# Half-height turns in large groups, inverse rows in another PSUM pool, and one forward transform with four residues

## Chip, core and metric

The kernel runs on one core of a Trainium2 chip. The metric is the device time of one execution in microseconds (us); of several runs the median counts. The engines are TensorE (PE in the profile, with PEld for its weight loads), VectorE (DVE), ScalarE (ACT), GpSimd (POOL) and SyncE (SP, which here issues DMAs only). PSUM, in which TensorE writes and from which ScalarE and VectorE read, has eight banks.

## What is computed

The reference is the forward pass of a gated block and the gradients of a loss with respect to nine of its inputs. With S = 2048 rows, D = 1024 channels and F = 3584:

```
xn = layernorm(q)                                  # 2048 x 1024
kv = shift_conv(k, shift_k) * v                    # 4 taps along the rows
y  = irfft(rfft(kv, 4096) * rfft(ssm_k, 4096))[:2048] + kv * ssm_D
g  = silu(((xn @ w_gate) * (xn @ w_up)) @ w_down)
out = q + (xn * y) * g
```

and then the gradients of q, k, v, shift_k, ssm_k, ssm_D, w_gate, w_up and w_down for a given gradient of out. All tensors are bf16.

## The kernel before

All work is on one core, in one program. TensorE does the large matrix products one after the other; the long convolution runs beside them, as pieces of work that are put between the matmuls.

**Forward stage (to about 513 us of the span).** The rows of q come in chunks, are normalised on VectorE, and are turned (transposed) on TensorE so that the channels lie on the partitions (`layer_norm`, L564 to L612; the last two chunks of four row blocks in `turn_late`, L614 to L619). `gu_unit` (L640 to L694) then does one unit: a slab of 256 columns of w_gate and w_up against four row blocks (two, or one, at the start). Each row block is eight matmuls of 512 columns into a PSUM tile `psg` (L656), which ScalarE copies to `gut` (L658). After a unit, VectorE multiplies the two halves into `hN` (in `multiply`), GpSimd stores hN, and `turn` (L684 to L694), deferred by five row blocks, turns the eight 128x128 blocks of hN with eight transposes on TensorE (L689) into one bank of `ps_tr`, ScalarE copies them to `hT` (L691), and SyncE stores 256 KB of hT to `HTd`. There are 14 slabs of four units.

A transpose here is a matmul: the block is loaded as weights, and the identity, 128 columns, streams through.

**Convolution (between the units).** `conv_forward` (L701 to L883) is a generator that is advanced by `tick` after every row block; the planner `make_pump` spreads its steps evenly by prices written beside each `yield`, which are DVE times less 0.95 of the TensorE time that the step adds (`pe_us`, `net`). Eight channel slices of 128 go through it. Per slice: two forward transforms, that of the filter h (with the D row added to it) and that of kv; a product in frequency; an inverse transform. A forward transform is done in two halves. A half is matmuls of 256 columns against a table into PSUM tiles `psF` (two buffers of two banks, pool `ps_cv`, L235), ScalarE copies of 1024 elements to `SP`, and sums and differences on VectorE. It exists in two forms: with four residues (`fwd4_half`, 16 matmuls a half; eight VectorE instructions of 1024 elements in all) and with eight (`fwd8_half` and `fwd8`, 8 matmuls a half; more VectorE instructions). `EIGHT` lists which (slice, kind) use the second; kind 0 is kv, kind 1 is h. The inverse ends in rows (`tail`): `inv8_rows` (L446) or `inv_rows` (L457) multiply two residues at a time into the single-bank tile `psY` (pool `ps_y`), ScalarE copies 512 elements to `yf` (L773), four times a slice. Before its transform, h of the next slice is turned by `h_rows` (L743 to L759): sixteen 128x128 blocks in two calls of eight (L752 and L754), each into the single buffer of `ps_tr`, each with a ScalarE copy (L755). The source of these blocks has a step of eight elements between columns. `turn_tables` (L186 to L195) turns the tables for the inverse, once.

**PSUM in this stage:** ps_y one bank, ps_tr one, psg two, and four for `ps_st` in the layer norm, which later become the two buffers of ps_cv.

**After it (513 us on).** The product with w_down (`bm_mm`, L994), the gates, and the last rows of the inverse of slice 7, whose four steps are put behind late matmuls 52, 55, 58 and 61 (`at`); then the whole backward pass, up to 1916 us. The order of instructions on each engine follows the program's order as a scheduler places it; instructions of the convolution on VectorE keep theirs.

Of the kernel before, what the change touches and what calls it, by code (L numbers as in the profile page):

```python
# [19 lines left out]
def build_kernel(  # L20
# [12 lines left out]
    P = 128  # L33
# [152 lines left out]
    def turn_tables(psp):  # L186

        for j in range(2):
            for rq in range(2):
                ps = psp.tile([P, 4, 2, P], BF16, name="psY")  # L190
                for i in range(4):
                    for k in range(2):
                        nc.tensor.transpose(ps[:, i, k, :], T4[j][:, 4 * rq + i, k, :], ident[:])
                nc.scalar.copy(out=TI[:, j, 4 * rq:4 * rq + 4], in_=ps[:])
                yield  # L195
# [253 lines left out]
    def inv_rows(G, psp, rp):  # L449

        ps = psp.tile([P, 2, 256], F32, name="psY")
        for i in range(2):
            r = 2 * rp + i
            n = 0
            for j in range(2):
                for k in range(2):
                    nc.tensor.matmul(ps[:, i, :], TI[:, j, r, k, :], gseg(G, r, j, k),  # L457
                                     start=(n == 0), stop=(n == 3))
                    n += 1
        return ps  # L460
# [67 lines left out]
    busy = ps_st.tile([P, 4, P], F32, name="tr")  # L528
# [35 lines left out]

    def layer_norm(b0, n, x4):
# [22 lines left out]
        for i in range(n):  # L588
            b = b0 + i
            q, qi = divmod(b, 4)  # L590
            last = V.tensor_scalar(x4[:, i, :], x4[:, i, :], mv[:, i, 0:1], RSTD[:, b:b + 1], op0=SUB, op1=MUL)
            if b < 2:
                for hh in range(2):
                    ps = ps_st.tile([P, 4, P], BF16, name="tr")
# [3 lines left out]
                    act_copy[0] = nc.scalar.copy(out=XNT[0][:, 4 * hh:4 * hh + 4, b * P:b * P + P], in_=ps[:])  # L598
# [10 lines left out]
            act_copy[0] = nc.scalar.copy(out=XNT[q][:, :, qi * P:(qi + 1) * P], in_=ps[:])  # L609
# [3 lines left out]
    def turn_late():  # L613
        for i, (x, q, qi) in enumerate(turn_rows):  # L614
            ps = ps_st.tile([P, DC, P], BF16, name="tr")
            for dc in range(DC):
                tr_ln[0] = nc.tensor.transpose(ps[:, dc, :], x[:, dc * P:(dc + 1) * P], ident[:])
            act_copy[0] = nc.scalar.copy(out=XNT[q][:, :, qi * P:(qi + 1) * P], in_=ps[:])
        turn_rows.clear()  # L619
# [4 lines left out]
    gu_mm = [None]  # L624

# [12 lines left out]
    chunk = [0]  # L638

    def gu_unit(sl, b0, n, w, tick):  # L640
# [26 lines left out]
        def multiply():  # L667
            with tc.issue_after(last.ins) if b0 + n <= 4 and chunk[0] <= 2 else nullcontext():
                by_half = lambda t: t.rearrange("p i (a f) -> p a i f", a=2)
                tt(hN[:, :, 0:n], by_half(gut[:, 0, 0:n]), by_half(gut[:, 1, 0:n]), MUL)  # L670
            st(Hd[sl][:, :, b0:b0 + n, :], hN[:, :, 0:n])
            defer(turn)
        hn[0] = multiply

        def store(hT):
# [3 lines left out]
            if n == 4:  # L679
                ht_st[0] = ld(to[q0:q0 + 2].rearrange("q f a s -> f q (a s)"), hT[:].rearrange("f q a i s -> f q (a i s)"))  # L680
            else:
                ht_st[0] = ld(to[q0, :, :, i0 * P:(i0 + n) * P], hT[:, 0, :, 0:n].rearrange("f a i s -> f a (i s)"))

        def turn():  # L684
            hT = fg.tile([P, 2, 2, 2, P], BF16, name="hT") if chunk[0] > 5 else lnp.tile([P, 2, 2, 2, P], BF16, name="hT_s", bufs=5)
            ps = ps_tr.tile([P, 2, 2, 2, P], BF16, name="tr")
# [3 lines left out]
            if n == 4:  # L690
                nc.scalar.copy(out=hT[:], in_=ps[:])  # L691
# [4 lines left out]
    h_out = []  # L696
    ht_st = [None]
    EIGHT = ((0, 0), (0, 1), (5, 0), (6, 0), (7, 0), (7, 1))
# [7 lines left out]
    def conv_forward():  # L706
# [36 lines left out]
        def h_rows(ds, c):  # L743
# [3 lines left out]
            if c == 0:  # L747
                S_["hx"] = cf.tile([P, NB, P], BF16, name="hx")
            pe_us[0] += 0.47
            ps = ps_tr.tile([P, 8, P], BF16, name="tr")  # L750
            with tc.issue_after(tr_ln[0].ins):
                nc.tensor.transpose(ps[:, 0, :], hrow[:, c, :, 0], ident[:])  # L752
            for r in range(1, 8):
                nc.tensor.transpose(ps[:, r, :], hrow[:, c, :, r], ident[:])  # L754
            nc.scalar.activation(S_["hx"][:, 8 * c:8 * c + 8, :], ps[:], ACT.Copy, scale=WSC)  # L755
            if c == 1:
                h_out.append(ds)
                if ds + 1 < 8:
                    load_h(ds + 1)  # L759
# [4 lines left out]
        def tail(ds):  # L764
# [5 lines left out]
            for rp in range(4):  # L770
                ps = (inv8_rows if ds in INV8 else inv_rows)(G, ps_y, rp)
                pe_us[0] += 0.45 if ds in INV8 else 0.9
                nc.scalar.copy(out=by_res(yf, rp), in_=rowps(ps))  # L773
                if ds == 7 and rp < 2:
                    nc.scalar.copy(out=y_first[0][:, 2 * rp:2 * rp + 2, 7 * P:8 * P], in_=yf[:, 2 * rp:2 * rp + 2])
                if rp == 3:
# [50 lines left out]
        h_rows(0, 0)  # L827
        h_rows(0, 1)
        yield 0.1
        tl = turn_tables(ps_y)  # L830
        sp = [half(0, S_["hx"], i, Dz[:, 0:P]) for i in range(2)]
        for ds in range(8):
# [16 lines left out]
            next(tl, None)  # L849
            room = cf.tile([P, 4, 256], F32, name="room", tag="hx")[:] if eight else None  # L850
            yield from transform(ds, int(ds > 0), sph, HX if ds else KX, room, nop1 if eight else lambda c: h_rows(ds + 1, c),
                                 lambda: next(tl, None))
            if ds == 0:
                S_["kst"] = st(KFd[0], KX[:])
            if eight:
                h_rows(ds + 1, 0)
            turned(HX, 1, 0, 1)
            yield 1.3
            if eight:
                h_rows(ds + 1, 1)  # L860
# [24 lines left out]
    F_TOTAL = 4 * SHIFT_W + 3.0 + 8 * (0.5 + FWD4_W + 1.3 + PROD_W + INV_W) + 10.0 - 0.95 * 8 * (4 * 1.75 + 0.95 + 4 * 0.9)  # L885
# [121 lines left out]
    ps_cv.release()  # L1007
    ps_bm = pool("ps_bm", 2, side="right", space=PSUM)
# [246 lines left out]
    def gate(b, ps, parts=None):  # L1255
# [23 lines left out]
        def turn():  # L1279
            ps = ps_tr.tile([P, DC, P], BF16, name=tr_name[0])  # L1280
            for dc in range(DC):
                nc.tensor.transpose(ps[:, dc, :], dbm[:, dc * P:(dc + 1) * P], ident[:])
            nc.scalar.copy(out=DBMT[b // 4][:, :, (b % 4) * P:(b % 4 + 1) * P], in_=ps[:])
# [53 lines left out]
    at = (52, 55, 58, 61)  # L1337
    for n in range(at[3] + 1):
# [27 lines left out]
    done = at[3] + 1  # L1366
# [35 lines left out]
    for p_ in (ps_bx, ps_tr, ps_y, ps_bm, mi, mo, mt, mh[1], mh[0]):  # L1402
# [364 lines left out]
```

## Time and profile before

| what | value |
|---|---|
| median of 3 runs | 1919.29 us (1917.67 to 1920.26) |
| profiled execution, span from first to last instruction | 1916.6 us |
| granted TensorE clock, mean | 1.000 |
| PE busy | 1905.7 us (99%), 10915 matmuls |
| DVE busy | 1557.1 us (81%) |
| ACT busy | 640.0 us (33%) |
| POOL busy | 334.5 us (17%) |

The span is 2.7 us shorter than the median of the runs. A row of a timeline gives the start of a group in us, its length, engine, line, operation, the tile written and read, the shapes and how many instructions were merged; a bracket at the end gives the engine's idle time before it and what ended that. Neighbouring matmuls overlap at their ends, so what one costs is the distance between the starts of two groups over the count of the first, not its length. In a row of stretches, each engine's busy time is followed by its number of instructions.

### The profile page before, as it was taken

To read this page: it belongs to the slowest core of one execution; us is meant where nothing else is said; L and a number is where in the kernel's file an instruction comes from. 1 tells how busy PE (TensorE), PEld (TensorE's weight loads), DVE (VectorE), ACT (ScalarE), POOL (GpSimd) and SP (SyncE) were. 2 spreads that over 40 slices of the span, in tenths; PEclk is the share of its full clock that TensorE was granted. 3 is DMA by queue.
4 is the path that set the end of the run, shared out by engine and by line. 5 is a ranking of instruction groups with operands and counts; after the bars stand their busy time and mean duration, and the time that the engine had idled before them with its cause. 6 is when DMAs were issued, how large, how long until landed. Compare 5 with 4: busy or idle time off the path is not lost. (4 is left out here: it accounts for less than half of the span.)

```text
span 1916.6 us, 27330 instructions
## 1 busy us (share of the span) xinstructions
PE 1905.7 (99%) x10915; PEld 1024.9 (53%) x10915; DVE 1557.1 (81%) x1723; ACT 640.0 (33%) x946; POOL 334.5 (17%) x465
## 2 busy tenths in 40 slices
PE   8999999999999999999999999999999999999999
PEld 5555555545544456666666665664444444444444
DVE  8999999999997556887999999999995205788862
ACT  5864555646433233432222222222222102011121
POOL 5121212111113220001031221111212101111120
PEclk9999999999999999999999999999999999999999
DMA  8776867668679997677887698585787999999962
GB/s 293 271 261 216 265 209 234 211 234 299 237 246 287 316 287 250 205 240 236 269 271 261 220 263 270 180 286 177 217 255 173 206 205 191 184 184 195 193 180 97
DMA packets 425487, 444.28 MB, mean 232 GB/s; under 512 B 268784, under 2 KB 343180, under 8 KB 410896
## 3 DMA queue, kind: packets, MB, share of 16 engines
q1 hardware_dynamic: 367888, 239.03, 46.9%
q0 software_dynamic: 41152, 174.15, 29.1%
q10 hardware_dynamic: 16320, 29.36, 4.1%
q8 instruction: 85, 1.39, 0.3%
q14 instruction: 42, 0.34, 0.1%
HBM read 193.87 MB, written 189.84 MB: 200 GB/s over the span
## 5 line engine op out<-in xcount | busy, mean ns | idle before, releaser
L656 PE MATMUL psg<-wslab,U 128*128 128x512 bf16 x1792 | 407.3, 379 | 3.0 <-DMA wslab<-in_B_w_gate_dram 2.0
L1458 PE MATMUL psb<-U,U 128*128 128x512 bf16 x1792 | 397.1, 379 | 0.0
L1603 PE MATMUL psx<-U,dgut 128*128 128x512 bf16 x1536 | 333.0, 379 | 0.5 <-DVE dxn L213 0.5
L1603 PEld LDWEIGHTS <-dgut 128*128 128x128 bf16 x1792 | 175.3, 98 | 212.1 <-issue 0.8
L1458 PEld LDWEIGHTS <-U 128*128 128x128 bf16 x1792 | 175.2, 98 | 198.0
L656 PEld LDWEIGHTS <-U 128*128 128x128 bf16 x1792 | 172.2, 98 | 187.4 <-issue 2.5
L1441 PE MATMUL psb<-wdt,U 128*128 128x256 bf16 x1792 | 205.6, 273 | 0.0
L213 DVE TENSOR_TENSOR W<-W 128x1024 f32<-128x1024 f32 (+1 forms) x192 | 189.1, 1001 | 4.2
L1441 PEld LDWEIGHTS <-U 128*128 128x128 bf16 x1792 | 175.3, 98 | 29.2
L1541 PE MATMUL psb<-U,U 128*128 128x512 bf16 x816 | 177.3, 379 | 0.0
L1463 ACT CAST wb<-psb 128x512 bf16<-128x512 f32 x112 | 65.6, 586 | 315.4 <-PE psb L1458 310.5
L1208 DVE SCALAR_TENSOR_TENSOR dkp<-dkT,kT 128x1024 bf16<-128x1024 bf16 (+2 forms) x64 | 78.3, 1224 | 104.0 <-DMA dkT<-DKSHd 102.2
L994 PE MATMUL psbm<-U,ht 128*128 128x512 bf16 x672 | 146.0, 379 | 0.0
L1541 PEld LDWEIGHTS <-U 128*128 128x128 bf16 x896 | 87.4, 98 | 104.3
L658 ACT CAST gut<-psg 128x512 bf16<-128x512 f32 x156 | 91.3, 588 | 120.0 <-PE psg L656 119.1
L1635 ACT ACTIVATE dx_t<-dxn 128x1024 bf16<-128x1024 f32 x15 | 15.9, 1057 | 324.2 <-DVE dxn L213 320.3
L994 PEld LDWEIGHTS <-ht 128*128 128x128 bf16 x672 | 65.6, 98 | 78.0
L213 DVE TENSOR_TENSOR U<-U,dht 128x2048 bf16<-128x2048 bf16 x56 | 68.3, 1221 | 46.4 <-ACT dht L1443 46.4
L1443 ACT CAST dht<-psb 128x512 bf16<-128x512 f32 x112 | 65.6, 587 | 116.3 <-PE psb L1441 116.3
L66 POOL DMA_DIRECT2D Hd<-hN x54 | 37.1, 686 | 292.3 <-DVE hN L213 289.4
L1582 ACT CAST wbs<-psb 128x512 bf16<-128x512 f32 x51 | 29.9, 586 | 145.4 <-PE psb L1541 137.3
L213 DVE TENSOR_TENSOR W<-SP 128x1024 f32<-128x1024 f32 x64 | 74.5, 1219 | 2.5 <-ACT SP L296 1.7
(261 smaller groups left out, 2386.3 us busy)
## 6 DMA issues: line engine op xcount, KB each, us to landing
U<-GUd SPq DMA_DIRECT2D x28, 1024.0 KB, 8.7
DGd<-U SPq DMA_DIRECT2D x28, 1024.0 KB, 6.5
GUd<-gut ACTq DMA_DIRECT2D x39, 512.0 KB, 5.5
out_dram<-wb SPq DMA_DIRECT2D x112, 128.0 KB, 4.8
U<-Hd SPq DMA_DIRECT2D x14, 1024.0 KB, 5.9
Hd<-hN POOLq DMA_DIRECT2D x54, 256.0 KB, 4.2
HTd<-hT SPq DMA_DIRECT2D x52, 256.0 KB, 3.9
ht<-HTd SPq DMA_DIRECT2D x18, 512.0 KB, 7.7
```

What stands on the lines that cost most here:

```text
L66: ins = nc.gpsimd.dma_start(out=out, in_=in_)
L213: pinned(V.tensor_tensor(o, a, b, op))
L656: gu_mm[0] = nc.tensor.matmul(ps[:], XNT[q][:, dc, qi * P:(qi + 1) * P], w[:, dc].rearrange("p a f -> p (a f)"), start=(dc == 0), stop=(dc ...
L658: nc.scalar.copy(out=gut[:, :, i], in_=ps[:].rearrange("p (a f) -> p a f", a=2))
L994: mm = nc.tensor.matmul(ps[:, dh * 512:(dh + 1) * 512], ht(fc)[:, i * P:(i + 1) * P], WD[fc // 4][:, fc % 4, dh * 512:(dh + 1) * 512], sta ...
L1208: ins = V.scalar_tensor_tensor(prod[:].rearrange("p r d -> p (r d)")[:, lo:H], dkT[:, 0, lo:H], 1.0, kT[:, 0, 13 + m + lo:13 + m + H], op0 ...
L1441: nc.tensor.matmul(ps[:, x * SLW:(x + 1) * SLW], DBMT[2 * hf + g][:, dc, (b % 4) * P:(b % 4 + 1) * P], wdt[:, dc, :], start=(dc == 0), sto ...
L1443: nc.scalar.copy(out=dht[:, 2 * e:2 * e + 2].rearrange("p b f -> p (b f)"), in_=ps[:])
L1458: nc.tensor.matmul(ps[:], XN[b // 4][:, b % 4, dc * P:(dc + 1) * P], dgus[b // 8][:, :, b % 8], start=(b == 0), stop=(b == NB - 1))
L1463: nc.scalar.copy(out=wb[:, dc % 2].rearrange("p a f -> p (a f)"), in_=ps[:])
L1541: nc.tensor.matmul(ps, h[:, f, b, :], DBM[b // 4][:, b % 4, dh * 512:(dh + 1) * 512], start=(b == 0), stop=(b == NB - 1))
L1603: nc.tensor.matmul(ps[:, dh * 512:(dh + 1) * 512], t[n][:, f, i * P:(i + 1) * P], WGU[n][:, f, dh * 512:(dh + 1) * 512], start=(n == 0 and ...
```

## The change

1. **Turns by halves of the rows.** A transpose of a 128x128 block becomes two of 64x128: partitions 0 to 63 and 64 to 127 are turned by two matmuls on separate halves of the array's rows, each with a 64x64 identity, so 64 columns stream through; the two results go to different banks. This is done where many turns stand together: hN of slabs 2 to 13, where the two units of a half of the rows are now kept (`mate`) and turned together as 16 blocks (`turn_pair`); all sixteen blocks of h in one call; and the 32 blocks of each late chunk (`turn_late`). `ps_tr` becomes two banks, still one buffer; hT becomes one buffer of double size, stored with one DMA of 512 KB.
2. **Inverse rows.** The pool ps_y goes. `inv_quad` does four residues at a time into a buffer of psF (after the end of ps_cv: into ps_tr), with ScalarE copies of 1024 elements, twice a slice. The tables are turned there too, in two groups of 16.
3. **kv of slice 5** leaves EIGHT and is transformed with four residues.
4. The last rows of slice 7, now two steps, stand behind late matmuls 62 and 69. The planner's price for TensorE of turning h goes from twice 0.47 to 0.67.

In number of instructions: 576 transposes of 128 columns become 1152 of 64, with as many weight loads; 16 matmuls of 256 columns are added; VectorE loses 10 tensor_tensor and 4 scalar_tensor_tensor of 512 elements and gains 2 tensor_tensor of 1024; 48 stores of hT become 24; 32 copies of inverse rows become 16.

```diff
     def turn_tables(psp):
...
-            for rq in range(2):
-                ps = psp.tile([P, 4, 2, P], BF16, name="psY")
...
+            ps = psp.tile([P, 8, 2, P], BF16, name="psT", tag="psF")
...
-    def inv_rows(G, psp, rp):
...
+    def inv_quad(G, ps, rq, eight):
+
+        for i in range(4):
+            r = 4 * rq + i
             n = 0
-            for j in range(2):
+            for j in range(1 if eight else 2):
                 for k in range(2):
...
-    ps_y = pool("ps_y", 1, space=PSUM)
...
-    ps_st = pool("ps_st", 4, space=PSUM)
...
+    ps_st = pool("ps_st", 1, space=PSUM)
+    turns = ps_st.tile([P, 4, 2, 4, P], BF16, name="tr")
...
+    def turn_halves(ps, src):
+
+        for hh in range(2):
+            rows = slice(64 * hh, 64 * hh + 64)
+            ins = nc.tensor.transpose(ps(hh), src[rows], ident[rows, rows])
+        return ins
...
     def turn_late():
+        ps = turns[:].rearrange("p (h j) i b x -> p h j i (b x)", h=2).rearrange("p h j i (a u) -> p h (j i) a u", u=64)
         for i, (x, q, qi) in enumerate(turn_rows):
-            ps = ps_st.tile([P, DC, P], BF16, name="tr")
             for dc in range(DC):
-                tr_ln[0] = nc.tensor.transpose(ps[:, dc, :], x[:, dc * P:(dc + 1) * P], ident[:])
...
+                tr_ln[0] = turn_halves(lambda hh: ps[:, hh, i, dc], x[:, dc * P:(dc + 1) * P])
...
+    def tr_tile():
+        return ps_tr.tile([P, 2, 8, P], BF16, name="tr")
...
-            defer(turn)
+            if sl < 2:
+                defer(turn)
+            else:
+                mate.append(hN)
+                if b0 % 8 == 4:
+                    defer(turn_pair)
...
+        def turn_pair():
+            hT = fg.tile([P, 4, 2, 2, P], BF16, name="hT", bufs=1)
+            two_, mate[:] = mate[0:2], mate[2:]
+            ps = tr_tile()[:].rearrange("p h b x -> p h (b x)").rearrange("p h (b u) -> p h b u", u=64)
+            for qq in range(4):
+                for a in range(2):
+                    for i in range(2):
+                        turn_halves(lambda hh: ps[:, hh, 4 * qq + 2 * a + i], two_[qq // 2][:, a, qq % 2 * 2 + i, :])
+            to = HTd[b0 // 8][sl // 4][:, :, 2 * (sl % 4):2 * (sl % 4) + 2, :]
+            for g in range(2):
+                nc.scalar.copy(out=halves(hT[:, 2 * g:2 * g + 2].rearrange("p q a i s -> p (q a i) s")), in_=ps[:, :, 8 * g:8 * g + 8])
+            ht_st[0] = ld(to.rearrange("q f a s -> f q (a s)"), hT[:].rearrange("f q a i s -> f q (a i s)"))
...
-    EIGHT = ((0, 0), (0, 1), (5, 0), (6, 0), (7, 0), (7, 1))
+    EIGHT = ((0, 0), (0, 1), (6, 0), (7, 0), (7, 1))
...
-        def h_rows(ds, c):
+        def h_rows(ds):
...
-            pe_us[0] += 0.47
-            ps = ps_tr.tile([P, 8, P], BF16, name="tr")
+            pe_us[0] += 0.67
+            ps = tr_tile()[:].rearrange("p h b x -> p h (b x)").rearrange("p h (b u) -> p h b u", u=64)
             with tc.issue_after(tr_ln[0].ins):
-                nc.tensor.transpose(ps[:, 0, :], hrow[:, c, :, 0], ident[:])
-            for r in range(1, 8):
-                nc.tensor.transpose(ps[:, r, :], hrow[:, c, :, r], ident[:])
-            nc.scalar.activation(S_["hx"][:, 8 * c:8 * c + 8, :], ps[:], ACT.Copy, scale=WSC)
...
+                turn_halves(lambda hh: ps[:, hh, 0], hrow[:, 0, :, 0])
+            for b in range(1, 16):
+                turn_halves(lambda hh: ps[:, hh, b], hrow[:, b // 8, :, b % 8])
+            for c in range(2):
+                nc.scalar.activation(halves(hx[:, 8 * c:8 * c + 8, :]), ps[:, :, 8 * c:8 * c + 8], ACT.Copy, scale=WSC)
...
-            for rp in range(4):
-                ps = (inv8_rows if ds in INV8 else inv_rows)(G, ps_y, rp)
...
+            for rq in range(2):
+                ps = (ps_tr if cv_gone else ps_cv).tile([P, 4, 256], F32, name="psI", tag="tr" if cv_gone else "psF")
+                inv_quad(G, ps, rq, ds in INV8)
...
-    at = (52, 55, 58, 61)
+    at = (62, 69)
```

More of the change, by code (lines that the diff above doesn't have):

```diff
@@ L188, in turn_tables @@
         for j in range(2):
-            for rq in range(2):
-                ps = psp.tile([P, 4, 2, P], BF16, name="psY")
[L191 to L195, printed above, removed]
+            ps = psp.tile([P, 8, 2, P], BF16, name="psT", tag="psF")
+            for r in range(8):
+                for k in range(2):
+                    nc.tensor.transpose(ps[:, r, k, :], T4[j][:, r, k, :], ident[:])
+            nc.scalar.copy(out=TI[:, j], in_=ps[:])
+            yield
     def pr(t, i, j):
@@ L638, in build_kernel @@
     chunk = [0]
+    mate = []
     def gu_unit(sl, b0, n, w, tick):
@@ L690, in turn @@
             if n == 4:
-                nc.scalar.copy(out=hT[:], in_=ps[:])
+                nc.scalar.copy(out=hT, in_=ps)
             else:
@@ L848, in conv_forward, with behind @@
                 S_["kst"] = st(KFd[ds], KX[:])
-            next(tl, None)
+            calls = []
+            def behind():
+                calls.append(0)
+                if len(calls) % 2 == 0:
+                    next(tl, None)
             room = cf.tile([P, 4, 256], F32, name="room", tag="hx")[:] if eight else None
-            yield from transform(ds, int(ds > 0), sph, HX if ds else KX, room, nop1 if eight else lambda c: h_rows(ds + 1, c),
-                                 lambda: next(tl, None))
+            yield from transform(ds, int(ds > 0), sph, HX if ds else KX, room, nop1 if eight else lambda c: h_rows(ds + 1) if c == 0 else None,
+                                 behind)
             if ds == 0:
@@ L1335, in late_mm @@
             return bm_mm(ps_of[b], hts[b // 2][0], b % 2, fc)
-    at = (52, 55, 58, 61)
-    for n in range(at[3] + 1):
+    at = (62, 69)
+    for n in range(at[1] + 1):
         mm = late_mm(n)
```

74 lines of the change are left out of this document (37 added, 37 removed).

## The prediction

> **What bounds the kernel now.** I read the totals first, then busy time by stage, then what PE waited for, and last single stretches of the timeline.
>
> ```profile
> PE 1905.7 (99%) x10915; PEld 1024.9 (53%) x10915; DVE 1557.1 (81%) x1723; ACT 640.0 (33%) x946; POOL 334.5 (17%) x465
> ```
> ```profile
> core 0: us, PE busy (x) PEld busy (x) DVE busy (x) ACT busy (x) POOL busy (x), PEclk, DMA share, GB/s
> 0.00:60.00 60.00, 54.11 (x402) 32.06 (x403) 51.72 (x122) 37.58 (x60) 28.15 (x44) 1.00 0.92 312
> 60.00:513.00 453.00, 452.20 (x2797) 250.15 (x2795) 447.06 (x422) 263.00 (x369) 76.02 (x108) 1.00 0.71 238
> 513.00:600.00 87.00, 86.94 (x419) 40.54 (x418) 81.03 (x110) 27.23 (x31) 18.39 (x28) 1.00 0.79 281
> 600.00:740.00 140.00, 139.94 (x777) 74.48 (x776) 67.88 (x102) 41.10 (x48) 26.48 (x42) 1.00 1.07 299
> 740.00:1460.00 720.00, 719.94 (x4410) 421.91 (x4408) 667.58 (x635) 201.38 (x337) 122.32 (x143) 1.00 0.76 233
> ```
>
> PE is busy in every stage, at full granted clock. The changed instructions lie between about 25 and 565 us. In the main part, 60 to 513 us, PE is busy for 452.20 of 453 us, but DVE for 447.06 too: two engines are full at once, and a gain on one of them alone is worth little. ACT has 263 of 453 and can be left out. From 600 us DVE is half idle.
>
> Busy could still hide waiting, so I look at the distance between starts.
>
> ```profile
> 298.80 0.82 PE L235 MATMUL psF<-kv,TF 128*128 128x256 bf16 x6
> 299.45 3.62 PE L656 MATMUL psg<-wslab,U 128*128 128x512 bf16 x16
> 302.91 0.61 PE L689 MATMUL tr<-ident,hN 128*128 128x128 bf16 x8
> 303.36 0.81 PE L656 MATMUL psg<-wslab,U 128*128 128x512 bf16 x3
> ```
>
> From start to start, 512 columns cost (302.91 - 299.45) / 16 = 0.216 us, 256 columns (299.45 - 298.80) / 6 = 0.108, and 128 columns (303.36 - 302.91) / 8 = 0.056. That is about 0.0025 us plus 0.417 ns a column, with weight loads hidden. So PE streams without gaps, and PE time removed here is real time, as far as DVE lets PE go ahead. The eight turns last 0.61 us though PE leaves them after 0.45: the pipe's tail is 0.16 us, normally covered by the next matmuls.
>
> **The change, part by part.** *Turns.* By that line, 64 columns cost 0.029 us. A block, now two halves, lies between 0.029 (side by side) and 0.058 us (one after the other). No half-height matmul is in this trace, nor a switch between whole and half array. I bound the switch by nothing and by the pipe's tail of 0.16 us, once on entering a group and once on leaving it. A group of 16 blocks is then between 16 x 0.029 = 0.46 and 16 x 0.058 + 0.32 = 1.25 us. I take 0.70: halves side by side, and one and a half tails. It is nearer the lower end because the halves use different rows, banks and weights, so that nothing in the data orders them.
>
> The Trainium skill, "TensorEngine Tiling (Array Packing)", section "Key Properties", says that a change of tiling mode drains TensorE; by that both tails are paid, and a group would be 0.78 by estimate. No run here shows it yet.
>
> Now 16 blocks of hN cost twice 0.45 = 0.90 us. Slabs 2 to 13 have 24 such groups (12 slabs, two halves of the rows): 24 x (0.90 - 0.70) = **4.8 us** less. For h:
>
> ```profile
> 319.18 1.03 PE L457 MATMUL psY<-HX,TI 128*128 128x256 bf16 x8
> 320.10 0.22 PE L752 MATMUL tr<-ident,U 128*128 128x128 bf16 x1
> 320.15 0.60 PE L754 MATMUL tr<-ident,U 128*128 128x128 bf16 x7
> 320.59 1.24 PE L656 MATMUL psg<-wslab,U 128*128 128x512 bf16 x5
> 321.87 0.22 PE L752 MATMUL tr<-ident,U 128*128 128x128 bf16 x1
> 321.92 0.59 PE L754 MATMUL tr<-ident,U 128*128 128x128 bf16 x7
> 322.35 1.67 PE L656 MATMUL psg<-wslab,U 128*128 128x512 bf16 x7
> ```
> ```profile
> 320.79 1.02 ACT L755 ACTIVATE hx<-tr 128x1024 bf16<-128x1024 bf16 x1
> ```
>
> The two calls take 0.49 and 0.48 us. Before the second, five matmuls end their share at 320.59 + 5 x 0.216 = 321.67, yet the turn starts at 321.87, just after ACT emptied the single buffer at 321.81: 0.2 us of waiting that the busy rows don't show. With both calls in one group of two banks this wait goes: 0.97 + 0.20 - 0.70 = 0.47 us, eight times, **3.8 us**. What is late next is the two ACT copies of a group (2.04 us) before the next user of ps_tr; 16 blocks come half as often, so I count nothing, with up to 0.5 us a slice the other way. The source is strided, which the weight loads feel:
>
> ```profile
> L689 PEld LDWEIGHTS <-hN x432: 95/98/98, 52.1 to 513.5; 128*128 128x128 bf16 x144
> ```
> ```profile
> L754 PEld LDWEIGHTS <-U x112: 142/148/158, 63.7 to 457.2; 128*128 128x128 bf16 x112
> ```
>
> A strided load lasts 148 ns against 98. Twice as many loads, no longer covered by 128 columns, might cost up to 16 x 0.062 x 2 + 0.32 = 2.3 us a group (0.49 / 8 is 0.062 a block); I stay at 0.70 and keep that for a rival. The planner's 0.67 for these blocks is a price in the program, not a row, and I take nothing from it.
>
> The late chunks:
>
> ```profile
> 48.85 1.95 PE L617 MATMUL tr<-ident,U 128*128 128x128 bf16 x32
> 50.63 1.67 PE L656 MATMUL psg<-wslab,U 128*128 128x512 bf16 x7
> ```
>
> 32 blocks in 1.78 us become 32 x 0.029 + 0.24 = 1.17: twice 0.6, **1.2 us**.
>
> *kv of slice 5.* 16 more matmuls of 256 columns, 16 x 0.108 = **1.7 us** of PE added. On DVE, by
>
> ```profile
> L213 DVE TENSOR_TENSOR W<-SP 128x1024 f32<-128x1024 f32 x64 | 74.5, 1219 | 2.5 <-ACT SP L296 1.7
> L284 DVE SCALAR_TENSOR_TENSOR HX<-W 128x512 bf16<-128x512 f32 x24 | 15.1, 685 | 0.2
> L213 DVE TENSOR_TENSOR W<-W 128x512 f32<-128x512 f32 x22 | 14.7, 688 | 0.3
> ```
>
> 14 instructions of 512 at 0.686 go and 2 of 1024 at 1.219 come: 9.6 - 2.4 = **7.2 us** less.
>
> *Inverse rows.* The same matmuls, in fewer and larger ACT copies, so nothing on PE. They now share psF with the forward halves. Each takes one of two buffers until its copy (about 1 us) is done; a half that follows at once would wait about that long. In the changed program's order at least one row block of matmuls (8 x 0.216 = 1.7 us) mostly stands between. Bounds: 0.5 us gained (short waits for the one-bank psY go) to 2 lost; I take 0. *Waiting mates:* the first hN of a pair waits a unit longer for its turn; with three hN buffers the next multiply still finds one free, so DVE doesn't wait. *Stores:* 24 of 512 KB for 48 of 256 KB; hT has one buffer, but
>
> ```profile
> HTd<-hT SPq DMA_DIRECT2D x52, 256.0 KB, 3.9
> ```
>
> 3.9 us to landing, even doubled, fits into the two units (2 x 4 x 8 x 0.216 = 13.8 us of matmuls) between groups. SP waits for each group's copies before it goes on, but half as often; the slab loads behind it have a slab's time. Nothing. *Late steps of slice 7:* PE work is moved, none added; putting them ten late matmul pairs on (10 x 2 x 0.216 = 4.3 us) gives DVE that much more time. Nothing.
>
> **Sum for PE:** -4.8 - 3.8 - 1.2 + 1.7 = -8.1 us. Of this 6.9 falls into the stretch where DVE is full, and DVE loses 7.2 there. So PE needs not run further ahead of DVE than now. How far it could is seen where PE's side needs a buffer that DVE empties:
>
> ```profile
> 306.85 4.63 DVE L213 TENSOR_TENSOR W<-SP 128x1024 f32<-128x1024 f32 x4
> ```
> ```profile
> 309.99 1.93 ACT L257 COPY SP<-psF 128x1024 f32<-128x1024 f32 x2 [0.65 <-PE psF L235]
> ```
>
> The first two of the four sums empty the SP that the copy at 309.99 fills; they end near 309.2, so 0.8 us is to spare there before ACT is late, and some 2 us more until two psF and two psg tiles are full and PE stops. DVE's own 7.2 plus about 3 us is therefore the most that this stretch can give.
>
> Against the profiled span: 1916.6 - 8.1 = 1908.5; the median lies 2.7 us above its span, and so do I: **1911 us**, 0.43% faster.
>
> **Rivals.**
> (a) *The halves cost less, and DVE caps the gain.* At 0.46 a group PE would save 24 x 0.44 + 8 x 0.71 + 2 x 0.85 - 1.7 = 16.2 us, but the 60 to 513 stretch gives only 7.2 + 3, with 1.7 ahead of it: 12 less, 1907 us. For: 447.06 of 453 on DVE. Against: needs switches for nothing.
> (b) *A floor under short matmuls.* If a half costs about as much however short, 0.025 us instead of less, side by side doesn't help: 32 x 0.025 = 0.80 and up to 0.32 for switches, 0.96 to 1.12 a group. Then hN loses 1.4 to 5.3, h gains 1.7 to 0.4, the late chunks gain 0.1 or lose 0.3, and with kv's 1.7 PE ends 1.3 to 6.9 us up: about 1923 us. Nothing in the trace is shorter than 128 columns, so it neither shows nor excludes it. That floor is an assumption close to the 0.029 of 64 columns alone. The Trainium skill, "TensorE: Matmul & The Clock Gate", section "Wait — 56ns, not 53.3ns?", states such a floor, 25 ns from start to start; its 56 ns at 128 columns agrees with this trace's 0.056, and its "Part 3: Packing small matmuls — row/col tiling" has matmuls on different row tiles 4 ns apart, which is for the forecast.
> (c) *One after the other, with the drains.* The two halves don't overlap, or a weight load has to wait until its rows are free. A group is 1.25 us: hN +8.4, h 8 x (1.30 - 1.17) = +1.0 (1.30: strided, 0.062 x 16 + 0.32; with loads doubled, up to +9), late chunks 2 x (1.86 + 0.32 - 1.78) = +0.8, kv +1.7: 12 us, **1931 us**, slower. It decides from the point where 16 blocks cost about 0.91 us with both switches: (24 x 0.90 + 8 x 1.17 + 2 x 1.78 - 1.7) / 36, what is paid now, less kv, over 36 times 16 blocks. For: each weight load of 98 ns is longer than 29 ns of columns; a load of whole height is hidden by a double buffer, which must also hold for halves. Against: loads of 98 ns already follow each other every 56 ns.
> (d) *DVE sets the pace, and new waits eat the rest.* If inverse rows in psF and the longer copies of ps_tr hold PE up by 0.5 us a slice each beyond what DVE's 7.2 us allow, 7.2 - 8 x 0.5 = 3.2 us stay: 1916 us.
>
> **How the numbers follow.** Forecast 0.55 (1908.5 to 1914), (a) 0.10, (b) 0.13, (c) 0.15, (d) 0.07. Shorter differences than 0.2% (3.8 us) can't be told from no change in a measurement of this kernel. Faster than 1915.5: the forecast, (a) and about half of (d), 0.68. Within: half of (d) and over half of (b), about 0.12. Slower than 1923.1: (c) and the rest of (b), 0.20. For the range, 1907 takes in (a); upwards it goes through (d) and half of (b) to 1922; left out are (c) and the upper end of (b), about 0.2.
>
> **What would show it.** In the profile after, 16 blocks of hN must lie about 0.7 us apart from the start of the group to the next matmul: below 0.55 is (a), 0.9 to 1.1 is (b), over 1.2 is (c). The turns of h should be one group per slice, without a wait inside. The main stretch should end near 505 us, with PE still full there; if PE stops before SP copies or psg, DVE was the cap. DVE should lose about 7 us before that point. From 600 us on everything should be the same, only earlier. The forecast is wrong if a group costs 0.91 us or more, or if the inverse rows in psF make forward halves wait by more than a microsecond a slice.

## The result and the profile after

| | before | after |
|---|---|---|
| median of 20 runs each | 1917.91 us | 1915.54 us |
| profiled execution, span | 1916.6 us | 1914.2 us |

The ratio is 0.9983 with a 95% interval of 0.9977 to 0.9989: 0.17% faster, 3.3 us by the ratio and 2.4 by the medians. The interval excludes 1, but the gain lies inside the 0.2% that the prediction had called too small to measure; with 20 runs of each it could be. The direction was right, the forecast of 8.1 us was not: less than half came.

The totals of the kernel after, and then the same stretches of busy time as before:

```profile
PE 1895.2 (99%) x11367; PEld 1014.8 (53%) x11507; DVE 1550.7 (81%) x1711; ACT 637.1 (33%) x927; POOL 334.8 (17%) x465
```
```profile
core 0: us, PE busy (x) PEld busy (x) DVE busy (x) ACT busy (x) POOL busy (x), PEclk, DMA share, GB/s
0.00:60.00 60.00, 51.60 (x438) 29.75 (x446) 48.81 (x120) 34.90 (x56) 27.45 (x43) 0.97 0.89 300
60.00:513.00 453.00, 449.83 (x3297) 243.01 (x3354) 445.94 (x414) 263.37 (x358) 77.22 (x109) 1.00 0.74 241
```

DVE lost 1557.1 - 1550.7 = 6.4 us, nearly as planned. PE's busy time can't be compared: the page has 11367 matmuls but 11507 weight loads, so some matmul records are missing and count as idle. What is new is in the first row: a granted clock of 0.97 where it was 1.00. That differs between executions: 15 of the 20 of the kernel after have a mean granted clock of 0.998 or 0.999 and a median of 1915.6 us, the other five have 1.000 and a median of 1913.9.

**Milestones on PE.** The same two points in both kernels, the first gate matmul after the first turn of four small hN blocks and the end of the gate matmuls (before, after):

```profile
39.99 3.61 PE L656 MATMUL psg<-wslab,U 128*128 128x512 bf16 x16 [0.59 <-ACT gut L658]
...
503.22 3.62 PE L656 MATMUL psg<-wslab,U 128*128 128x512 bf16 x16
506.67 0.60 PE L446 MATMUL psY<-HX,TI 128*128 128x256 bf16 x4
```
```profile
43.83 1.46 PE L673 MATMUL psg<-wslab,U 128*128 128x512 bf16 x6 [1.21 <-ACT gut L675]
...
505.40 3.62 PE L1032 MATMUL psbm<-U,U 128*128 128x512 bf16 x16
```

So the start became 43.83 - 39.99 = **3.8 us slower**, and the stretch from there **5.1 us faster** (461.57 for 466.68). At 505.4 us 1.3 us are left. Another 1.1 us is gained behind it; 0.5 of that is a wait for DVE after 600 us, the only one of PE there in before (psx for dxn), and gone in after. For the remaining 0.6 no cause was found.

**The groups.** A group of hN and one of h in the kernel after:

```profile
113.74 1.24 PE L673 MATMUL psg<-wslab,U 128*128 128x512 bf16 x5
114.91 0.64 PE L571 MATMUL tr<-ident,hN 64*128 64x64 bf16 x32
115.49 0.82 PE L673 MATMUL psg<-wslab,U 128*128 128x512 bf16 x2
```
```profile
146.82 0.81 PE L673 MATMUL psg<-wslab,U 128*128 128x512 bf16 x3
147.56 1.17 PE L571 MATMUL tr<-ident,U 64*128 64x64 bf16 x32
148.66 1.04 PE L673 MATMUL psg<-wslab,U 128*128 128x512 bf16 x3
```

For hN: 115.49 - 114.91 = 0.58 from the first turn to the next matmul, and before it the five gate matmuls end their share at 113.74 + 5 x 0.216 = 114.82, 0.09 ahead of the turn. So a group costs 0.67 us; forecast was 0.70. For h the same reading gives 1.10 + 0.09 = 1.19 us, and before it was 0.97 + 0.20 = 1.17: nothing gained. The other groups agree: from first turn to next matmul the 24 of hN take 0.57 us at the median, and all eight of h 1.09 or 1.10. The weight loads tell the difference (minimum, median and maximum in ns; from 60 to 513 us, where no loads of the late chunks are among those of h):

```profile
L571 PEld LDWEIGHTS <-hN x768: 92/95/96, 114.9 to 511.4; 64*128 64x128 bf16 x192
...
L571 PEld LDWEIGHTS <-U x256: 137/163/173, 67.4 to 451.4; 64*128 64x128 bf16 x128
```

**The start.** PE in before and then in after:

```profile
25.67 1.99 PE L608 MATMUL tr<-ident,U 128*128 128x128 bf16 x32 [0.95 <-DVE U L591]
27.50 1.67 PE L656 MATMUL psg<-wslab,U 128*128 128x512 bf16 x7
```
```profile
18.04 5.78 PE L673 MATMUL psg<-wslab,U 128*128 128x512 bf16 x26
27.00 0.62 PE L620 MATMUL tr<-ident,U 128*128 128x128 bf16 x8 [3.19 <-DVE U L603]
...
29.36 1.06 PE L620 MATMUL tr<-ident,U 128*128 128x128 bf16 x8 [0.22 <-ACT gut_s L675]
```

Before, the 32 turns of a chunk were one run. After, they are four groups of eight with other work between; PE waits 3.19 us for the normalised rows where it waited 0.95, and the clock drops behind that wait (of the last three numbers the first is the clock; before had 1.00 in both stretches):

```profile
25.00:30.00 5.00, 2.77 (x21) 1.93 (x23) 4.56 (x15) 2.46 (x5) 1.39 (x3) 0.79 0.23 86
30.00:35.00 5.00, 5.00 (x39) 2.87 (x38) 4.70 (x14) 3.14 (x5) 1.41 (x3) 0.87 0.70 238
```

Part of the wait comes from DVE, which normalises these rows 1.3 us later (PE's turn starts at 27.00 for 25.67). In after its first statistics of them wait for a load, to 18.63 where they start at 18.28 in before, and a multiply that in before stands ahead of them, at 17.25, now stands behind the first ones and delays the rest by about 1.0:

```profile
18.63 1.88 DVE L584 BATCH_NORM_STATS2 bst<-U 128x6 f32<-128x512 bf16 x3 [2.00 <-DMA U<-in_A_q_dram]
20.43 1.04 DVE L212 TENSOR_TENSOR hN_s<-gut_s 128x256 bf16<-128x256 bf16 x1
```

In the code, four single-bank tiles of `ps_st` became one tile `turns` of four banks. That is in the diff, and the prediction gave it no term.

**The theory to test.** (1) hN by halves in groups of 16 brings its share; (2) h by halves brings nothing, because its weights are strided; (3) the layer norm's single tile of four banks costs the start; (4) kv of slice 5 costs PE a little and is needed, since DVE would otherwise hold PE up. **The rivals:** the main stretch is held by DVE, so that it gives about 5 us whatever PE saves; the start is slower by chance or because of the halves in the late chunks; kv alone makes the kernel faster, as DVE was the bound already.

### The profile page after: what moved, and what is told of

It reads as the page before. It is cut to its first block, busy times and chain, and to the rows that moved or that the text cites. A ratio compares the mean times of both kernels' runs of the same rounds, so it can differ in the third digit from the quotient of the medians.

```text
span 1914.2 us, 28265 instructions
## 1 busy us (share of the span) xinstructions
PE 1895.2 (99%) x11367; PEld 1014.8 (53%) x11507; DVE 1550.7 (81%) x1711; ACT 637.1 (33%) x927; POOL 334.8 (17%) x465
## 4 chain that ended last, share of the span: by engine, by line
PE 96%; DVE 1%; issue 1%; ACT 1%; DMA 1%; SPq 0%; ACTq 0%; DVEq 0%
PE psb L1497 20%; PE psx L1642 20%; PE psg L673 19%; PE psb L1480 10%; PE psb L1580 9%; PE psbm L1032 9%; PE psF L234 3%; PE tr L571 1%; PE psI L455 1%; PE psY L1191 1%; PE psY L445 1%; PE psx L1580 1%; DMA U<-in_A_q_dram 1%; ACT U L631 0%; DVE bst L584 0%
## 5 line engine op out<-in xcount | busy, mean ns | idle before, releaser
L673 PE MATMUL psg<-wslab,U 128*128 128x512 bf16 x1728 | 399.0, 380 | 5.2 <-ACT gut L675 1.2
```

What stands on the lines that cost most here:

```text
L673: gu_mm[0] = nc.tensor.matmul(ps[:], XNT[q][:, dc, qi * P:(qi + 1) * P], w[:, dc].rearrange("p a f -> p (a f)"), start=(dc == 0), stop=(dc ...
```

## The experiments

Each is the kernel after with one edit, unless said otherwise. Medians are of 5 to 11 runs; the ratio is against runs of the kernel before taken beside them, whose median was 1917.46 to 1917.58 (1917.91 in the table above). e2, e4, e5, e6, e9, e10 and e11 have the start of after, which loses its clock in some executions and not in others. So a difference of medians against after can hold up to 1.7 us (1915.6 less 1913.9) that is not the edit's; where it matters, executions of like mean clock are compared as well.

**e1: the layer norm's turns as before** (four single-bank tiles, the late chunks by whole blocks).

```diff
-    ps_st = pool("ps_st", 1, space=PSUM)
-    turns = ps_st.tile([P, 4, 2, 4, P], BF16, name="tr")
+    ps_st = pool("ps_st", 4, space=PSUM)
...
-                tr_ln[0] = turn_halves(lambda hh: ps[:, hh, i, dc], x[:, dc * P:(dc + 1) * P])
+                tr_ln[0] = nc.tensor.transpose(ps[:, dc, :], x[:, dc * P:(dc + 1) * P], ident[:])
```

> The changed kernel with the layer norm's turns as before: four single-bank tiles, and the late chunks turned in whole blocks. Theory (start): the first 45 us of the changed kernel lose 3.8 us because all four banks are one tile, so that each turn waits for the copy of the turn before it; undone, the first 45 us are as before, the late chunks lose about 0.6 us again, and the time falls by about 3 us, to about 1912.5 us (ratio to before about 0.997). Rival: the loss is scatter of the loads of q in one execution; then only the 0.6 us show, and it is 1916 us.

Measured: 1912.01 us, ratio 0.9972 [0.9962, 0.9983]. The milestone of the start is back:

```profile
35.00 1.99 PE L623 MATMUL tr<-ident,U 128*128 128x128 bf16 x32 [0.73 <-DVE U L597]
36.83 2.32 PE L666 MATMUL psg<-wslab,U 128*128 128x512 bf16 x10
...
39.96 3.61 PE L666 MATMUL psg<-wslab,U 128*128 128x512 bf16 x16 [0.59 <-ACT gut L668]
...
501.67 3.62 PE L1025 MATMUL psbm<-U,U 128*128 128x512 bf16 x16
```

39.96 is before's 39.99, and the gate matmuls end at 501.67, 3.7 us earlier than in after. The start's loss belongs to these edits. By the medians what is gained there is kept to the end (3.5 us); the profiled execution itself was the slowest of seven, with a wait of 2.0 us for a load behind 600 us. All seven have a mean clock of 1.000, and 1912.01 is 1.9 us below the five executions of after that have it too. So about half of the 3.5 us is the clock that the start of after mostly loses.

**e2: h whole, in one group of 16.**

```diff
...
             for b in range(1, 16):
-                turn_halves(lambda hh: ps[:, hh, b], hrow[:, b // 8, :, b % 8])
+                nc.tensor.transpose(ps[:, b // 8, b % 8], hrow[:, b // 8, :, b % 8], ident[:])
```

> The changed kernel with the sixteen blocks of h turned whole, still in one group and two banks. Theory (strided loads): a half-height turn of h costs 0.069 us a block because its two strided weight loads don't fit behind 64 columns; whole blocks cost 0.062, and the group falls from 1.19 us with its two switches to about 0.98 without any: 8 x 0.21 = 1.7 us less, about 1914 us. Rival: DVE is the cap, PE time is worth nothing there, and it stays at 1915.5 us.

Measured: 1914.03 us, 0.9977 [0.9967, 0.9987], 1.5 us below after, and 1.4 where the mean clock is 1.000 in both (1912.5 for 1913.9; three executions and five).

```profile
146.66 0.22 PE L787 MATMUL tr<-ident,U 128*128 128x128 bf16 x1
146.72 1.09 PE L789 MATMUL tr<-ident,U 128*128 128x128 bf16 x15
147.65 1.67 PE L673 MATMUL psg<-wslab,U 128*128 128x512 bf16 x7
```

147.65 - 146.66 = 0.99 us for the group, 0.2 less than by halves, eight times: 1.6. So with this stride whole blocks are the cheaper ones, and what the single group was to gain for h (the wait for ACT) is gained only this way.

**e5: the same halves of h, but from neighbouring columns.** It changes the order of the filter's rows, that is, what is computed; the work is the same.

```diff
+            hflat = U[5][:, 0:2048]
...
-                turn_halves(lambda hh: ps[:, hh, b], hrow[:, b // 8, :, b % 8])
+                turn_halves(lambda hh: ps[:, hh, b], hflat[:, b * P:(b + 1) * P])
```

> The changed kernel, but the blocks of h are taken as 128 neighbouring columns instead of every eighth, so that the weight loads have unit step; the filter's rows are then in another order, which changes the values of the convolution and nothing else. Theory (strided loads): the group falls from 1.19 to the 0.67 us of hN, 8 x 0.52 = 4.2 us less, about 1911.5 us if DVE lets PE run on, with the group's length the sure sign. Rivals: the turns of h are slow for another reason (group stays at 1.19 us, 1915.5 us); or they get shorter and DVE caps the stretch (group 0.67 us, time down by under 2 us, PE waiting before SP copies).

Measured: 1911.85 us, 0.9969 [0.9958, 0.9981], 3.7 us below after, but 2.7 where the mean clock is 1.000 in both (1911.2 for 1913.9; three executions and five).

```profile
145.85 0.64 PE L571 MATMUL tr<-ident,U 64*128 64x64 bf16 x32
146.43 1.90 PE L673 MATMUL psg<-wslab,U 128*128 128x512 bf16 x8
```
```profile
L571 PEld LDWEIGHTS <-U x384: 92/95/97, 36.7 to 446.6; 64*128 64x128 bf16 x192
```

The loads last 95 ns (those of the late chunks among them) instead of 163, and the group is 0.58 like hN's. The stride is the whole cause. It also speaks against the first rival: PE could save another 4 us in this stretch. Here, though, the view of waits has a first trace of DVE's limit, at the last hN turn:

```profile
PE tr L571 <- DVE hN L212: 0.8, 1, 0.8
```

**e6: hN whole, still 16 blocks to a group.**

```diff
-                        turn_halves(lambda hh: ps[:, hh, 4 * qq + 2 * a + i], two_[qq // 2][:, a, qq % 2 * 2 + i, :])
+                        nc.tensor.transpose(ps[:, qq // 2, qq % 2 * 4 + 2 * a + i], two_[qq // 2][:, a, qq % 2 * 2 + i, :], ident[:])
...
```

> The changed kernel with the sixteen blocks of hN turned whole, still in one group of two units. Theory (halves side by side): the group goes from 0.67 to 0.90 us, 24 x 0.23 = 5.4 us more, about 1921 us, slower than before the change. Rival: the gain is the grouping's and the single waits', not the halves'; then it stays at about 1916 us.

Measured: 1921.45 us, 1.0018 [1.0009, 1.0027], 5.9 us above after; 24 x (0.90 - 0.67) = 5.5. Without this part the change would have been slower than before.

**e3: e1 and e2 together**, to see whether the two gains add.

> The changed kernel with both of the first two edits: the layer norm's turns as before, and h turned in whole blocks in one group. Theory (two separate losses on PE): they add up, -3.5 and -1.5 us, about 1910.5 us, ratio 0.9964. Rival (DVE caps the main stretch once PE is so far ahead): about 1912, no better than the first of the two alone.

Measured: 1910.73 us, 0.9961 [0.9949, 0.9973]: 4.8 us below after, for 3.5 + 1.5. They add.

**e8: e3, and the late chunks by halves in single-bank tiles** (two row blocks at a time, each half into a tile of its own).

```diff
+            pss_ = [ps_st.tile([P, 2, DC, 64], BF16, name="tr") for hh in range(2)]
+            for k, (x, q, qi) in enumerate(two_):
+                for dc in range(DC):
+                    tr_ln[0] = turn_halves(lambda hh: pss_[hh][:, k, dc], x[:, dc * P:(dc + 1) * P])
...
```

> As the run with both edits, and the late chunks turned by halves again, but in single-bank tiles (two tiles per two row blocks, one per half). Theory: the second late chunk, which doesn't wait for DVE, falls from 1.78 to some 1.15 us, the first stays at DVE's pace: 0.6 us less than with both edits, about 1910 us. Rival: copies that wait for two row blocks instead of one hold the next unit up, and it is no faster or up to 1 us slower.

Measured: 1910.21 us, 0.9959 [0.9947, 0.9971]. That is 0.5 us below e3, which these runs don't tell apart for certain. It settles a point of e1, which had undone two things: with halves in the late chunks, but single banks, the start is as before (the milestone is at 40.08), so the halves are not what cost it.

```profile
34.88 1.78 PE L565 MATMUL tr<-ident,U 64*128 64x64 bf16 x64 [0.72 <-DVE U L597]
36.81 2.11 PE L671 MATMUL psg<-wslab,U 128*128 128x512 bf16 x9 [0.16 <-issue]
```

The first late chunk takes 1.93 us by halves, where e1's whole blocks took 1.83 (35.00 to 36.83): its rows arrive from DVE one block after the other, so that shorter turns have to wait for them. This is the fastest version of the study, 0.4% below the kernel before.

**e4: kv of slice 5 back at eight residues**, as before the change.

```diff
-    EIGHT = ((0, 0), (0, 1), (6, 0), (7, 0), (7, 1))
+    EIGHT = ((0, 0), (0, 1), (5, 0), (6, 0), (7, 0), (7, 1))
```

> The changed kernel with kv of slice 5 back at eight residues: 16 matmuls less on PE (1.7 us), 7.2 us more on DVE. Theory (DVE caps, as the prediction has it): PE would be some 7 us further ahead of DVE than before the change, with room for about 3; the gain in the main stretch is lost beyond that, about 1917.5 us, with PE waiting before SP copies. Rival (DVE's lag is taken up after 513 us, where DVE is not full): PE's 1.7 us are gained, about 1914 us.

Measured: 1922.89 us, 1.0023 [1.0015, 1.0032], 7.4 us above after, although PE has 16 matmuls less. PE around the last hN turn, and the clock by stretches:

```profile
508.66 0.41 PE L571 MATMUL tr<-ident,hN 64*128 64x64 bf16 x16
514.54 0.61 PE L571 MATMUL tr<-ident,hN 64*128 64x64 bf16 x16 [5.47 <-DVE hN L212]
```
```profile
508.00:514.00 6.00, 1.07 (x20) 0.41 (x18) 5.86 (x9) 0.00 (x0) 0.55 (x1) 0.82 0.99 357
514.00:518.00 4.00, 3.24 (x22) 1.50 (x24) 3.97 (x5) 1.93 (x2) 0.67 (x1) 0.50 0.52 201
518.00:524.00 6.00, 6.00 (x31) 3.05 (x30) 5.96 (x9) 1.01 (x1) 0.00 (x0) 0.94 0.69 218
```

This is DVE's cap. PE does not fall behind bit by bit; apart from waits of 0.6 us and less (1.6 us in all) it runs ahead through the whole stretch and then stops once, because the last turn needs the last hN, which stands in DVE's queue behind the sums of the transforms. In after the same place has room of 1.0 us:

```profile
509.27 0.68 DVE L212 TENSOR_TENSOR hN<-gut 128x1024 bf16<-128x1024 bf16 x1
```
```profile
510.99 0.64 PE L571 MATMUL tr<-ident,hN 64*128 64x64 bf16 x32
```

The multiply ends at 509.95, the turn starts at 510.99. With 6.4 us more on DVE, 6.4 - 1.0 = 5.4 us of wait are due, and 5.47 came. After the wait PE pays twice, since the clock stands at 0.50 and then 0.94: from 514.54 on, 3.46 x 0.50 + 6 x 0.06 = 2.1 us. Less 1.7 us for the 16 matmuls, wait and clock make 5.9 of the 7.4 us, and the short waits are about the rest.

**e11: e4, with the last hN turn behind 32 matmuls of the next product instead of 16**, to test that this one place is the cap.

```diff
-    with tc.issue_after(bm_first(range(4)).ins):
+    with tc.issue_after(bm_first(range(8)).ins):
...
-    fc_ = 4
+    fc_ = 8
```

> The run with kv of slice 5 at eight residues, with the last group of hN put behind 32 instead of 16 matmuls of the next stage. Theory (DVE's cap acts at this one turn, which waited 5.5 us for the last hN): some 4 of the 5.5 us come back, about 1919 us, less what the later loads of the rest of w_down may cost (up to 2 us, as they start after this turn). Rival (the cap is spread over the stage): it stays at 1923 us.

Measured: 1915.11 us, 0.9989 [0.998, 0.9997], 7.8 us below e4 and, by the medians, level with after. 16 matmuls are 3.5 us, yet the wait fell by 4.4, and the lost clock came back too:

```profile
PE tr L571 <- DVE hN L212: 1.1, 1, 1.1
```
```profile
508.00:514.00 6.00, 4.86 (x56) 2.71 (x55) 5.89 (x8) 1.92 (x3) 1.23 (x2) 1.00 0.94 369
```

4.4 of the wait and 2.1 of the clock are 6.5 of the 7.8 us. The other 1.3 us are not settled; the clock at the start, lost in the profiled execution of e4 and kept in that of e11, can make as much. So in this stretch DVE's work has only one due time that matters. The four residues for kv of slice 5 and a later turn are two ways to meet it. Where the mean clock is 1.000 (eight of e11's eleven executions, five of after's 20), the later turn is the dearer one by 1.0 us (1914.95 for 1913.93); its last turn still waits 1.1 us.

**e7: the kernel before, with only kv of slice 5 at four residues.**

```diff
-    EIGHT = ((0, 0), (0, 1), (5, 0), (6, 0), (7, 0), (7, 1))
+    EIGHT = ((0, 0), (0, 1), (6, 0), (7, 0), (7, 1))
```

> The kernel before with kv of slice 5 at four residues, alone. Theory (before the change PE sets the pace and DVE keeps up): 16 matmuls of 256 columns more, 1.7 us, about 1919.3 us; DVE's 7 us bring nothing by themselves. Rival (DVE holds PE up before the change already): it gets faster, 1915 us or less.

Measured: 1918.51 us, 1.0006 [0.9998, 1.0015]: 1.05 us above before by the medians, with 1.7 expected and nothing excluded between -0.4 and 2.9. It is not faster, so DVE did not hold PE up in the kernel before; the third rival is out.

**e9: halves, but eight blocks to a group**, to weigh the switch between whole and half array.

```diff
-                mate.append(hN)
-                if b0 % 8 == 4:
-                    defer(turn_pair)
+            defer(turn)
...
+                for i in range(8):
+                    turn_halves(lambda hh: ps[:, hh, i], hN[:, i // 2 % 2, i // 4 * 2 + i % 2, :])
```

> The changed kernel with hN turned by halves in groups of one unit (eight blocks) instead of two. Theory (each group pays about 0.19 us for its two switches): 48 groups of 8 x 0.030 + 0.19 = 0.43 us instead of 24 of 0.67: 24 x 0.19 = 4.6 us more, about 1920 us, nearly what whole blocks take. Rival: the switches are hidden in small groups as the pipe is then shorter; it stays within 1 us of 1915.5.

Measured: 1927.99 us, 1.0054 [1.0041, 1.0068], 12.5 us above after, far too much, and for another reason: hT had one buffer, which now had to be stored after every group. The view of waits:

```profile
ACT hT L720 <- DMA HTd<-hT: 25.5, 10, 5.0
```

ACT stood still for 25.5 us in ten waits, so the run says nothing of the switch. **e10** is e9 with two buffers of hT.

```diff
-            hT = fg.tile([P, 4, 2, 2, P], BF16, name="hT", bufs=1)[:, 0:2] if chunk[0] > 5 else ...
+            hT = fg.tile([P, 2, 2, 2, P], BF16, name="hT")[:] if chunk[0] > 5 else ...
```

> The run with groups of one unit again, now with two buffers of hT, since ScalarE waited for the stores of the one buffer (21.6 us in nine places) in the run before. Theory (switches of 0.19 us a group): 48 groups of 0.44 instead of 24 of 0.67 us, 24 x 0.21 = 5 us over the changed kernel, about 1920.5 us. Rival: the single buffer had nothing to do with it and small groups cost what the run before showed, about 1928 us.

Measured: 1920.04 us, 1.0012 [1.0003, 1.0021], 4.5 us above after.

```profile
109.78 5.56 PE L673 MATMUL psg<-wslab,U 128*128 128x512 bf16 x25
115.27 0.41 PE L571 MATMUL tr<-ident,hN 64*128 64x64 bf16 x16
115.61 2.76 PE L673 MATMUL psg<-wslab,U 128*128 128x512 bf16 x12
```

A group of eight blocks takes 0.34 us, one of sixteen 0.58, so a block costs (0.58 - 0.34) / 8 = 0.030 us, and 0.10 us remain for leaving the half array; with the 0.09 ahead of each group a switch there and back costs **0.19 us**. 48 x 0.43 - 24 x 0.67 = 4.6 us is what was measured. The size of the groups decides: a block costs 0.056 whole, so 0.19 / (0.056 - 0.030) = 7.3 blocks are needed to win anything.

**e12: everything whole, with the layer norm as before.** What is left of the change is the inverse rows in psF, the groups of 16, the larger stores and kv.

> The changed kernel with all turns in whole blocks and the layer norm's turns as before: what is left is the inverse rows in the transforms' PSUM, the large groups, and kv of slice 5. Theory (each part has its PE price and they add): 1.7 up for kv, some 2 down for the single waits of h and some short waits of the inverse rows, about 1917 us; against the run with both edits it lacks the halves of hN, 24 x 0.23 = 5.4 us. Rival (the inverse rows in the forward transforms' buffers cost waits): over 1919 us.

Measured: 1916.94 us, 0.9996 [0.9987, 1.0005], 6.2 us above e3. These parts together cost nothing and bring next to nothing. It agrees with what PE waited for in after from 60 to 600 us, a single entry:

```profile
PE psbm L1032 <- issue: 0.2, 1, 0.2
```

No wait for psF in 540 us.

## Why the prediction came out half right

- **hN, -4.8:** right, and for the reason given. A group is 0.67 us, not 0.70; the trace gives 24 x 0.23 = 5.5, e6 5.9 and e3 against e12 6.2.
- **h, -3.8: this term of the sum failed.** It measured nothing: 1.19 us a group for 1.17. The prediction saw the strided loads (148 ns for 98), worked out that they could set the pace, and then wrote "I stay at 0.70 and keep that for a rival". In the rival it was combined with halves that don't overlap, so the case that came true had no price: halves side by side, paced by strided loads. A block takes 1.10 / 16 = 0.069 us in halves; without the 0.10 for leaving the half array, if that is as for hN, it is 0.063, which is the 0.062 of a whole strided block. So the halves won nothing, and the switch of 0.19 is what makes the group dearer than e2's (1.19 for 0.99). Of the 0.47 a group, the 0.20 of waiting for ACT was real (e2 brings it back), the width was not (e5).
- **Late chunks, -1.2: half came.** The second, in after

```profile
52.78 1.11 PE L571 MATMUL tr<-ident,U 64*128 64x64 bf16 x64
53.82 1.90 PE L673 MATMUL psg<-wslab,U 128*128 128x512 bf16 x7
```

went from 1.78 to 1.04 + 0.1 us (0.6). The first is paced by DVE's normalisation (e8); the stretch to 60 us in before, where PE is idle for 6 us, could have told that PE work saved there need not be time saved.
- **The start, +3.8: this step was missing.** Change 1 was costed by its matmuls only; that four tiles of a bank became one tile of four banks went unread. e1 shows the price, e8 that the halves are not to blame. The price is not one number. In e6 and e11, which have the same start, the profiled execution kept a clock of 1.00 from 25 to 35 us, and the milestone is 1.2 and 1.8 us behind before:

```profile
41.21 3.61 PE L673 MATMUL psg<-wslab,U 128*128 128x512 bf16 x16 [1.21 <-ACT gut L675]
```
```profile
41.80 3.61 PE L673 MATMUL psg<-wslab,U 128*128 128x512 bf16 x16 [1.21 <-ACT gut L675]
```

In the six that lost the clock there (after, e2, e4, e5, e9, e10) it is at 42.86 to 43.83, with after's the latest. How it comes about is in part argued: each turn into the shared tile is put behind the ACT copy of the one before it, so that the chunk's turns fall apart into four groups, other work moves between and the long wait at 24 us arises. The rows of after fit the first step (the third and fourth group start at 31.84 and 33.55, the copies before them end at 31.46 and 33.50); that this makes the wait, and moves DVE's multiply, no run shows by itself. With e1's edits both are gone.
- **kv of slice 5, +1.7 on PE, -7.2 on DVE:** 1.05 by e7 (1.7 is inside its interval) and 6.4.
- **Inverse rows, waiting mates, stores, late steps, 0:** right (e12; no wait in 540 us). A store takes 4.1 us to landing, twice as large, where it took 3.9.

- **The cap by DVE:** size right, place wrong. "DVE's own 7.2 plus about 3 us" was to be the most that the stretch gives. In e5,

```profile
42.86 3.40 PE L673 MATMUL psg<-wslab,U 128*128 128x512 bf16 x15 [1.21 <-ACT gut L675]
...
500.54 3.62 PE L1033 MATMUL psbm<-U,U 128*128 128x512 bf16 x16
```

it gives 466.68 - (500.54 - 42.86) = 9.0 us, and there the first wait of 0.8 us appears. But PE does not stop at SP copies or psg: it stops at the last hN turn, where after has 1.0 us left.
- **The sum** of the stretch in after: -5.5 (hN) + 0.2 (h) - 0.6 (second late chunk) + 1.7 (kv) = -4.2, measured -5.1; for the other 0.9 there is no term. With the start's 3.8, -1.3 is left at 505 us.
- **The rivals:** (a) needed switches for nothing, and they cost 0.19. (b) asked for 0.025 us a half, 0.80 a group of 32; the group takes 0.58, so there is no such floor between halves on different rows. (c) and (d) are refuted by the 0.67 of a group and by the missing waits.

## What to carry to other kernels

Before costing a narrower matmul, check what paces it: if its weight loads are strided, the loads do, and splitting the rows doubles their number: here a strided block took 0.063 us in halves and 0.062 whole. Half-height turns pay only in large groups of contiguous blocks, here above 7 blocks; the switch costs 0.19 us however many there are. Read the tile declarations of a diff as closely as its instructions: one tile over several banks instead of several tiles cost two thirds here of what the best part of the change gained, about half of it through the clock that PE's wait lost in most executions.

## What the runs showed of the hardware

- A strided weight load of half height (step of eight elements) lasts 163 ns at the median, a contiguous one 95; with two of them to a block, a block takes 0.063 us against 0.030, the switch left out of both.
- The change between whole and half array costs 0.09 us going in and 0.10 coming out. The Trainium skill, "TensorEngine Tiling (Array Packing)", section "Key Properties", says that a change of tiling mode drains TensorE; the trace agrees in kind, with less than the tail of 0.16 us each that the prediction's estimate took.
- A PE that stood idle for 5.5 us (e4) had a granted clock of 0.50 from 514 to 518 us, 0.64 in the next 1 us and 1.00 in the one after, so it was at full clock some 4 us after it resumed; 3.2 us of idleness (after, at 24 us) already left 0.79 and 0.87 in two stretches of 5 us. About that length it is not the wait alone that decides. At the start, the view of waits has a wait of 2.6 us in e4 and of 2.7 in e11 for the same normalised rows, and the stretch from 25 to 30 us that follows has a clock of 0.72 in e4 and of 1.00 in e11. The Trainium skill, "TensorE: Matmul & The Clock Gate", section "What's actually happening", puts the fall to half clock after an idle window of about 3.4 us, and says that the window runs freely. That the wait of 5.5 us lost the clock agrees with the first; that 2.6 us lost it and 2.7 did not fits the second, though 2.6 is shorter than the window stated. A wait of 5.5 us on a full PE cost 1.4 times itself here, 5.5 + 2.1.
